# Column totals by one all-ones product, an earlier weight load and a finer deal of one block's second product, in an attention and mixture-of-experts kernel

## The chip, the cores and the metric

The kernel runs on one core of a Trainium2 chip. The metric is the device time of one execution in microseconds (us); lower is better. Most of what follows concerns three of the core's engines: TensorE (PE in the profile; its weight loads are shown apart, as PEld), VectorE (DVE) and ScalarE (ACT). PE multiplies matrices into PSUM; DVE and ACT do elementwise work and empty PSUM; POOL and SP here mostly issue DMA transfers (70 of POOL's 82 instructions in the profile before).

The mean granted TensorE clock of a run was 0.996 to 1.000. In the two stretches of time by which I judge below (stages A and B) it was 1.00 in the profiles before and after, and in every profile the first twenty 512-column products of stage A took 4.48 us and a pair of 384-column products in stage B 0.48 to 0.50 us, so it explains no difference there; in whole times it has a small share. Kernels that were timed in rounds have runs of the state "fast"; four kernels got a single look each, whose state is unknown, and I use their traces and not their whole times.

## The reference, cut to what matters

An attention with linear cost gives `x` (4608 tokens of 512 numbers). Then comes a mixture of eight experts, whose gates are made by the Sinkhorn normalisation. Eight times, rows and then columns of a 4608x8 matrix are scaled to fixed sums:

```python
logits = x @ w_gate
P = np.exp(logits - logits.max())
for _ in range(8):
    P /= P.sum(1, keepdims=True) + 1e-09
    P /= P.sum(0, keepdims=True) + 1e-09
    P *= N / E
out = np.zeros((N, D))
for e in range(E):
    h = np.maximum(x @ w1[e], 0.0)
    out += P[:, e:e + 1] * (h @ w2[e])
```

A row of `P` is one token, and a row sum needs only that token's eight numbers. A column sum runs over all tokens. On the chip the tokens lie over 128 partitions, 36 on each, so a column sum is first a sum within each partition (`colp`, 128x8) and then one across partitions, which this kernel gives to PE, as a product with ones.

## The kernel before: the parts that matter

The kernel has three stages. Attention and expert 0 run together over blocks of 512 tokens (blocks 0 to 6). In blocks 7 and 8 attention is over, expert 0 goes on, and the Sinkhorn normalisation runs beside it. From then on experts 1 to 7 run with a scheme of fewer products (sums of weights and of tokens are made by DVE so that seven products replace eight); there PE is nearly always busy (9.97 to 10.00 us of each 10 us window from 220 to 960 us, before).

The Sinkhorn normalisation is a generator: each `yield` hands back to the loop that issues PE's main work, so its pieces are dealt between other products. DVE works through its instructions in the order in which they are written (in the changed kernel a reciprocal that is written behind an add-relu starts at 195.41 us, behind the add-relu of 194.94, though its product began at 193.41; where it is written ahead, in scaled_at_once, it starts at 192.53, 0.43 us after its product), so where a `yield` stands decides what DVE has to do first.

```python
def sinkhorn():
    small = (W2[:, 0:E], W2[:, TCH - E : TCH])          # a borrowed PSUM bank
    for it in range(8):
        rs = ...; ve.reduce_sum(out=rs[:], in_=P_tok[:], axis=AX.X)
        rr = ...; ve.reciprocal(out=rr[:], in_=rs[:])
        yield
        ve.tensor_tensor(out=P_tok[:], ... rr ..., op=ALU.mult)
        colp = sk_pool.tile([P, E], FP32, name="colp")
        ve.reduce_sum(out=colp[:], ...)
        yield
        for step in tw_steps[it][:2]: step()            # sums of expert 1's weights
        yield
        tot_ps = small[0][0:1, :]                       # totals on one partition
        te.matmul(out=tot_ps, lhsT=ones_col[:], rhs=colp[:], start=True, stop=True)
        t2 = sk_pool.tile([1, E], FP32, name="t2")
        ve.reciprocal(out=t2[:], in_=tot_ps)
        for step in tw_steps[it][2:]: step()
        yield
        te.matmul(out=small[1], lhsT=scale_row[0:1, ...], rhs=t2[0:1, :], ...)  # to all
        ve.tensor_tensor(out=P_tok[:], ... small[1] ..., op=ALU.mult)
        yield
```

Sums of expert 1's first weights (`tw_steps`, four sets of four DVE instructions) ride along in iterations 3 to 6. In blocks 7 and 8, by slots of one 128-row product, and then in the fills of expert 1's first groups, the pieces are dealt so:

```python
for j in range(B - 1, NJ):                        # blocks 7 and 8
    tiles = halves(hT, w0, ...)                   # second product, each tile in 2 parts
    for slot in range(NS):
        if slot < FT: ffn1(hT, w0, j, [slot])     # first product
        elif j < NJ - 1: next(tiles)              # block 7: its second product too
        else: break
        ...
        if j == NJ - 1:                           # block 8
            if slot == 0: sums_x = x_sums(1, xs_first[1])
            next(sums_x, None)                    # four sums of tokens, for unit 1
        ... balanced(...)                         # pieces of Sinkhorn

def start_fill():                                 # 28 fills in expert 1's first groups
    if k_fill % 7 in (0, 3): next(tiles, None)    # block 8's second product
    if k_fill % 6 != 1: balanced(1)               # one piece of Sinkhorn
    k_fill += 1
```

When the last part of a tile is done, ACT or DVE, in turn, copies the 128x512 result from PSUM to `acc`.

## Time and profile before

| | before |
|---|---|
| median of 4 runs (those of the first comparison) | 983.02 us |
| profiled span | 980.3 us |
| PE busy | 967.1 us, 99% |
| DVE, ACT busy | 82%, 58% |

The first part of the page gives each engine's busy time, its share of the span and its instructions; the fourth part gives the chain of work that ended last, by engine:

```profile
PE 967.1 (99%) x7871; PEld 674.9 (69%) x7871; DVE 806.6 (82%) x1834; ACT 564.3 (58%) x1262; POOL 60.6 (6%) x82
...
PE 94%; DVE 2%; ACT 2%; DMA 1%; POOL 0%; issue 0%; ACTq 0%; SPq 0%; POOLq 0%
```

PE bounds the kernel nearly everywhere. What is left are the gaps on PE. From 222 us on there are hardly any before the last 20 us, so the change can win only in the hand-over to expert 1. I cut that hand-over in two by marks that every version has. Stage A runs from the first gate product of block 7 (`p_ps<-wg,xT`) to the first marking product (`copied_ps<-xT`, made when a PSUM bank is lent). Stage B runs from there to the second marking product. The start of both is the start of a record on PE's timeline, so the durations are exact to a few hundredths.

Lines of PE's timeline of the kernel before follow. The columns are start, length, engine, line, operation, output and inputs, shapes, count; in brackets stands the idle time before, and what ended it.

```profile
165.64 0.65 PE L109 MATMUL p_ps<-wg,xT 128*128 128x8 f16 x20
...
188.82 0.38 PE L109 MATMUL copied_ps<-xT 128*128 128x512 f16 x1
...
193.60 0.48 PE L109 MATMUL h_ps<-S,w1e 128*128 128x384 f16 x2 [0.41 <-ACT u L109]
...
199.62 0.20 PE L109 MATMUL copied_ps<-colp,ones_col 128*1 128x8 f32 x2 [1.20 <-DVE colp L109]
...
204.79 0.20 PE L109 MATMUL copied_ps<-colp,ones_col 128*1 128x8 f32 x2 [0.78 <-DVE colp L109]
...
210.41 0.38 PE L109 MATMUL copied_ps<-xT 128*128 128x512 f16 x1
```

Stage A takes 188.82 - 165.64 = 23.18 us, stage B 210.41 - 188.82 = 21.59 us. In B, PE waits 1.20 and 0.78 us for `colp`, DVE's sums within partitions. Two more waits for ACT (0.41 shown, and 0.24 at 210.1, both for `u`, a copy of an intermediate sum that ACT takes out of PSUM) and one of 0.15 in A make 2.78 us in both stages.

### The profile page before, as it was taken

What the parts mean: (1) busy time and instruction counts of PE and PEld (TensorE: products, weight loads), DVE (VectorE), ACT (ScalarE), POOL (GpSimd) and SP (SyncE); (2) the same over time, 40 slices, a digit from 0 to 9 for tenths busy, and PEclk for the clock granted to TensorE, in tenths of its full rate; (3) what the DMA queues carried; (4) which work ended last, traced back from release to release, by engine and by line L of the source; (5) the groups of instructions that cost most, each with busy time, mean ns of one, the idle gap of its engine ahead of it and who ended that gap; (6) DMA issues with size and microseconds to landing.
All of it is one profiled execution on the core that took longest, in us unless ns stands there. A gap on an engine that the chain in (4) does not pass through costs nothing.

```text
span 980.3 us, 20270 instructions
## 1 busy us (share of the span) xinstructions
PE 967.1 (99%) x7871; PEld 674.9 (69%) x7871; DVE 806.6 (82%) x1834; ACT 564.3 (58%) x1262; POOL 60.6 (6%) x82
## 2 busy tenths in 40 slices
PE   9999999989999999999999999999999999999997
PEld 6545444457777777777777777777777777777775
DVE  7767774788989888988888888988888888988887
ACT  5767665467776555555555555555555555555551
POOL 6231110010000000000000000000000000000001
PEclk9999999999999999999999999999999999999999
DMA  9999881730113400223103401223103401104435
GB/s 165 184 158 172 150 134 28 145 65 33 42 33 68 93 25 25 60 59 66 49 25 69 92 25 28 63 58 66 46 25 76 85 25 34 40 26 120 127 87 129
DMA packets 80336, 73.54 MB, mean 75 GB/s; under 512 B 33264, under 2 KB 72176, under 8 KB 80240
## 3 DMA queue, kind: packets, MB, share of 16 engines
q0 software_dynamic: 27232, 30.94, 20.2%
q1 hardware_dynamic: 52768, 41.06, 16.9%
q8 instruction: 61, 1.00, 0.4%
q14 instruction: 35, 0.29, 0.1%
q10 hardware_dynamic: 240, 0.26, 0.1%
HBM read 83.12 MB, written 12.98 MB: 98 GB/s over the span
## 4 chain that ended last, share of the span: by engine, by line
PE 94%; DVE 2%; ACT 2%; DMA 1%; POOL 0%; issue 0%; ACTq 0%; SPq 0%; POOLq 0%
PE rows_ps L109 34%; PE h_ps L109 28%; PE copied_ps L109 11%; PE p_ps L109 11%; PE y_ps L109 6%; PE small_ps L109 4%; DMA acc_hi<-q_p 1%; ACT hT L109 0%; ACT acc_lo L109 0%; DVE acc_hi L927 0%; POOL hs_last L942 0%; DVE P_tok L109 0%; DMA out_dram<-acc_lo 0%; DVE colp L109 0%; ACT u L109 0%
## 5 line engine op out<-in xcount | busy, mean ns | idle before, releaser
L927 DVE SCALAR_TENSOR_TENSOR acc_lo<-rows_ps,P_tok,acc_lo 128x512 f32<-128x512 f32 (+1 forms) x322 | 203.0, 639 | 74.4 <-PE rows_ps L109 74.3
L109 PEld LDWEIGHTS <-H 128*128 128x128 f16 x2080 | 203.0, 98 | 83.1 <-issue 1.2
L863 ACT CAST u<-h_ps 128x384 f16<-128x384 f32 x288 | 137.6, 478 | 131.2 <-PE h_ps L109 131.2
L109 PEld LDWEIGHTS <-w1e 128*128 128x128 f16 x1632 | 156.4, 98 | 66.4 <-issue 6.3
L857 DVE CUSTOM_DVE_ANT_0 H<-p_ps,u 128x384 f16<-128x384 f32 x329 | 180.8, 549 | 7.0 <-PE p_ps L109 6.6
L109 PEld LDWEIGHTS <-hs 128*128 128x128 f16 x1500 | 146.5, 98 | 56.2
L109 PE MATMUL h_ps<-S,w1e 128*128 128x384 f16 x672 | 164.1, 326 | 1.1 <-ACT u L109 0.9
L109 PE MATMUL p_ps<-xT,T 128*128 128x384 f16 x672 | 164.1, 326 | 0.1
L109 PE MATMUL rows_ps<-V,H 128*128 128x256 f16 x1000 | 150.0, 273 | 0.7 <-DVE acc_hi L927 0.7
L109 PE MATMUL h_ps<-xT,w1e 128*128 128x384 f16 (+1 forms) x616 | 150.0, 350 | 0.1
L109 PE MATMUL rows_ps<-w2e,hs 128*128 128x256 f16 x1000 | 150.0, 273 | 0.0
L895 ACT ACTIVATE H<-h_ps 128x384 f16<-128x384 f32 x144 | 70.6, 490 | 95.1 <-PE h_ps L109 95.1
L109 PEld LDWEIGHTS <-T 128*128 128x128 f16 x1008 | 98.1, 98 | 29.3 <-issue 2.8
L109 PE MATMUL rows_ps<-w2e,H 128*128 128x256 f16 (+1 forms) x568 | 91.2, 285 | 0.0
L876 ACT COPY copied_ps<-h_ps 128x384 f32<-128x384 f32 x144 | 67.5, 469 | 35.3 <-PE h_ps L109 35.3
L886 ACT ACTIVATE H<-copied_ps 128x384 f16<-128x384 f32 x144 | 70.8, 492 | 20.4 <-PE copied_ps L109 20.4
L109 PE MATMUL h_ps<-S,T 128*128 128x384 f16 x336 | 81.8, 325 | 0.3 <-ACT copied_ps L109 0.3
L109 PE MATMUL copied_ps<-xT,w1e 128*128 128x384 f16 x336 | 82.1, 326 | 0.0
L109 PE MATMUL copied_ps<-w2e,H 128*128 128x256 f16 x504 | 75.5, 272 | 0.0
L109 PE MATMUL rows_ps<-V,hs 128*128 128x256 f16 x500 | 75.0, 272 | 0.0
L927 DVE SCALAR_TENSOR_TENSOR acc_lo<-copied_ps,P_tok,acc_lo 128x256 f32<-128x256 f32 x126 | 60.0, 476 | 0.5
L927 DVE SCALAR_TENSOR_TENSOR acc_hi<-rows_ps,P_tok,acc_hi 128x512 f32<-128x512 f32 (+1 forms) x56 | 41.2, 736 | 20.5 <-PE rows_ps L109 19.7
(147 smaller groups left out, 950.0 us busy)
## 6 DMA issues: line engine op xcount, KB each, us to landing
S<-x_saved SPq DMA_DIRECT2D x108, 192.0 KB, 2.4
out_dram<-acc_lo SPq DMA_DIRECT2D x62, 128.0 KB, 2.4
w1e<-in_moe_w_dram POOLq DMA_DIRECT2D x7, 1024.0 KB, 8.9
w2e<-in_moe_w_dram POOLq DMA_DIRECT2D x7, 1024.0 KB, 9.7
q_ld<-in_q_dram POOLq DMA_DIRECT2D x16, 288.0 KB, 6.4
k_ld<-in_k_dram POOLq DMA_DIRECT2D x16, 288.0 KB, 8.2
v_ld<-in_v_dram POOLq DMA_DIRECT2D x16, 288.0 KB, 9.4
x_saved<-S SPq DMA_DIRECT2D x18, 192.0 KB, 1.9
```

The source lines that it names most:

```text
L109: i = getattr(self.engine, name)(*args, **kwargs)
L857: latest = ve._custom_dve(TENSOR_ADD_SAT, out=out, in0=ps[:, 0:TU], in1=t[:], s0=FP32_MAX, s1=0.0)
L863: se.copy(out=t[:], in_=ps[:, 0:TU])
L876: se.copy(out=Y[:, 0:TU], in_=X[:, 0:TU])
L886: se.activation(out=h11, in_=Y[:, 0:TU], func=AF.Relu)
L895: se.activation(out=h12, in_=X[:, 0:TU], func=AF.Relu)
L927: ve.scalar_tensor_tensor(out=a, in0=rows, scalar=P_tok[:, g, self.e : self.e + 1], in1=a, op0=ALU.mult, op1=ALU.add,)
```

## The change

It has three parts, with three intents. The totals are made with a 128x128 matrix of ones, so that every partition has them at once: one product per iteration instead of two, and no reciprocal on a single partition in between. Expert 1's weights take the place of the input buffers, which come free long before the buffer `hT` that they replaced until now; so their sums can be made two iterations earlier. The last block's second product is dealt in quarters of a tile and not in halves. The diff, cut to its core:

```diff
     with ExitStack() as p1:
-        hA = p1.enter_context(tc.tile_pool(name="hA", bufs=1))
-        cs_pool = p1.enter_context(tc.tile_pool(name="cs_pool", bufs=1))
         ld = p1.enter_context(tc.tile_pool(name="ld", bufs=4))
         ...
+        cs_pool = p1.enter_context(tc.tile_pool(name="cs_pool", bufs=1))
+        hA = p1.enter_context(tc.tile_pool(name="hA", bufs=1))
 ...
-        scale_row = const.tile([1, 2, P], FP32, name="scale_row")
+        ones_all = const.tile([P, P], FP32, name="ones_all")
+        ve.memset(ones_all[:], 1.0)
 ...
-            tot_ps = small[0][0:1, :]
-            te.matmul(out=tot_ps, lhsT=ones_col[:], rhs=colp[:], start=True, stop=True)
-            t2 = sk_pool.tile([1, E], FP32, name="t2")
-            ve.reciprocal(out=t2[:], in_=tot_ps)
+            te.matmul(out=total, lhsT=ones_all[:], rhs=colp[:], start=True, stop=True)
             for step in tw_steps[it][2:]:
                 step()
             yield
-            te.matmul(out=small[1], lhsT=scale_row[...], rhs=t2[0:1, :], ...)
-            ve.tensor_tensor(out=P_tok[:], in0=P_tok[:], in1=small[1]..., op=ALU.mult)
+            t2 = sk_pool.tile([P, E], FP32, name="t2")
+            ve.reciprocal(out=t2[:], in_=total)
+            ve.scalar_tensor_tensor(out=P_tok[:], in0=P_tok[:], scalar=<N/E or N/E/XS>,
+                in1=t2[:]..., op0=ALU.mult, op1=ALU.mult)
 ...
-        tw, tw_steps[3 + i] = w1_steps(w_next, i)
+        tw, tw_steps[1 + i] = w1_steps(w_next, i)
 ...
-        tiles = halves(hT, w0, [...])
+        tiles = dealt(hT, w0, [...], 2 if j < NJ - 1 else 4)
 ...
-        if k_fill % 7 in (0, 3):
+        if k_fill % 7 in (0, 2, 3, 5):
             next(tiles, None)
```

More of the change, by code (lines that the diff above doesn't have):

```diff
@@ L310 @@
         ve.memset(ones_col[:], 1.0)
-        scale_row = const.tile([1, 2, P], FP32, name="scale_row")
-        ve.memset(scale_row[:, 0, :], float(N) / float(E))
-        ve.memset(scale_row[:, 1, :], float(N) / float(E) / XS)
+        ones_all = const.tile([P, P], FP32, name="ones_all")
+        ve.memset(ones_all[:], 1.0)
         eps_row = cs_pool.tile([1, 32], FP32, name="eps_row")
@@ L1023, in sinkhorn @@
     def sinkhorn():
-        small = (W2[:, 0:E], W2[:, TCH - E : TCH])
+        total = W2[:, 0:E]
         for it in range(8):
@@ L1050, in sinkhorn @@
             yield
-            te.matmul(
-                out=small[1], lhsT=scale_row[0:1, 1 if it == 7 else 0, :], rhs=t2[0:1, :],
-                start=True, stop=True,
-            )
-            ve.tensor_tensor(
+            t2 = sk_pool.tile([P, E], FP32, name="t2")
+            ve.reciprocal(out=t2[:], in_=total)
+            ve.scalar_tensor_tensor(
                 out=P_tok[:], in0=P_tok[:],
-                in1=small[1].unsqueeze(1).to_broadcast([P, NG, E]), op=ALU.mult,
+                scalar=float(N) / float(E) / (XS if it == 7 else 1.0),
+                in1=t2[:].unsqueeze(1).to_broadcast([P, NG, E]),
+                op0=ALU.mult, op1=ALU.mult,
             )
@@ L1063, in balanced, with dealt @@
             next(balance, None)
-    def halves(hT, w, tiles):
+    def dealt(hT, w, tiles, parts):
         for i, (c0, g) in enumerate(tiles):
-            for part in range(2):
+            for part in range(parts):
                 ffn2(
                     hT, w, c0, g, rows2[i % 3][:],
-                    range(part * FT // 2, (part + 1) * FT // 2),
+                    range(part * FT // parts, (part + 1) * FT // parts),
                 )
@@ L1101 @@
         hT = next_h()
-        tiles = halves(hT, w0, [(ts * P, j * TCH // P + ts) for ts in range(TCH // P)])
+        tiles = dealt(
+            hT, w0, [(ts * P, j * TCH // P + ts) for ts in range(TCH // P)],
+            2 if j < NJ - 1 else 4,
+        )
         for slot in range(NS):
```

## The prediction

> **What bounds the kernel.** TensorE. The page of the kernel before has PE busy 99% of 980.3 us at a granted clock of 0.999; the chain that ended last is 94% PE. From 222 to 960 us every 10 us window shows PE at 9.97 to 10.00, and the change touches nothing there. All it can win lies at the hand-over from attention and expert 0 to expert 1, 163 to 215 us. PE's timeline there has seven idle gaps, 3.36 us together:
>
> - 2.13 us wait for DVE's part of the Sinkhorn normalisation (0.15 at 186.8, 1.20 at 199.6, 0.78 at 204.8);
> - 0.41 us at 193.6 waits for ACT's snapshot `u`, behind the copy of a finished tile to `acc_hi`;
> - 0.82 us at 210 to 214 waits for ACT, which then multiplies gates.
>
> **What the change does there.**
>
> 1. *Totals.* Each of 8 iterations has a 128x1 f32 product (0.12 us on the chain) and a 1x128 one (0.31 us); after each the next four 512-column products take 0.97 us, not 0.86. The first pair goes: (0.12 + 0.11) x 8 = 1.8 us of PE. The other will load 128x128 f32 weights. [...] I keep the 182 ns that the trace shows for the 1x128 load (80 ns for 128x1). A PE-DVE-PE trip goes too; DVE's reciprocal (192 ns) and multiplication (451 ns) should keep their size.
> 2. *Weights.* Expert 1's load lies in bytes that the last attention inputs free, not under `hT`. Their last DVE readers run at 140 to 145 us; now the load issues at 166.8. It should issue at 141 to 146 and land by about 156, where DMA is little used. By itself this saves nothing: the first weight sums start at 184.5, after landing. It lets the sums move from iterations 3 to 6 to 1 to 4. Each set is 0.28 + 0.29 + 0.23 + 0.27 = 1.07 us of DVE, so some 2 to 2.5 us leave 189 to 206 us, where DVE is nearly full. I estimate an iteration there at 2.65 us of Sinkhorn, 1.1 of add-relu and part of a 0.69 copy, some 4.0 us, against 4.1 of PE work; with the sums it was about 5. That is the 1.2 and 0.8 us of wait.
> 3. *Quarters.* The same products as 16 pieces of 0.43 us instead of 8 of 0.86. It evens PE's filler between a column sum and its total, and moves the tile copies from a group's fourth fill to its sixth, where ACT's snapshot isn't waiting.
>
> **Sum on the critical path.** Small products 1.8 us, DVE waits 2.13 to about 0.6 (1.5 us), ACT's copy about 0.2; the 0.82 us of gates stay. Some 3.3 us, or 0.3%. I predict 979.7 us, range 978.0 to 982.0. Faster by over 2%: 0.005; within 2%: 0.985; slower: 0.01.
>
> **What would show each step right.** Eight pairs of f32 products instead of sixteen, at about 0.3 us each. POOL's issue of `w1e` near 141 us, weight sums starting near 172 us, none after about 190. PE's waits for `colp` under 0.7 us in total. No tile copy ahead of a PE wait for `u`. After 222 us everything as before, 3 us earlier.
>
> **What would make it wrong.** The 128x128 f32 load or product costing more than the 1x128 one; the early load delaying the last transposes by DMA (3.4 us to landing) until the denominators at 149 us wait; weight sums in block 7 delaying DVE's evictions; the load still waiting for the attention stage's end, so that DVE stalls on it at 172 us; the four gates on ACT moving to a worse place.

## The result, and the profile after

The median fell from 983.02 us to 981.12 us (four runs each, 980.48 to 981.30 after, 982.31 to 985.69 before). The ratio is 0.9975, with a 95% interval of 0.9955 to 0.9994. Ratios here are the mean time of one kernel's runs over the mean time of the other's runs of the same rounds, so not quite the ratio of the medians that I quote. The gain of the medians is 1.9 us where I had predicted 3.3; the time is inside the predicted range, and the interval of the ratio leaves room for a gain of 0.6 to 4.4 us.

The same lines as before, from the page of the changed kernel:

```profile
PE 964.4 (99%) x7855; PEld 674.2 (69%) x7855; DVE 807.1 (82%) x1833; ACT 565.2 (58%) x1262; POOL 60.6 (6%) x82
...
PE 88%; DMA 4%; DVE 3%; issue 2%; ACT 1%; POOL 1%; POOLq 0%; ACTq 0%; SPq 0%
```

The chain's shares moved, but this is not the change at work in stages A and B: ahead of 66 us the chain now runs through early loads (`k_ld`, `w1e`, `w2e`). It does so in weights_alone (below) too, which is not faster. PE is busy 99% in both.

And from PE's timeline of the changed kernel, both gate and marking products and the waits in between:

```profile
165.98 0.64 PE L109 MATMUL p_ps<-wg,xT 128*128 128x8 f16 x20
...
187.44 0.38 PE L109 MATMUL copied_ps<-xT 128*128 128x512 f16 x1
...
189.77 0.39 PE L109 MATMUL copied_ps<-colp,ones_all 128*128 128x8 f32 x2 [1.20 <-DVE colp L109]
...
193.41 0.39 PE L109 MATMUL copied_ps<-colp,ones_all 128*128 128x8 f32 x2 [0.32 <-DVE colp L109]
...
198.25 0.39 PE L109 MATMUL copied_ps<-colp,ones_all 128*128 128x8 f32 x2 [0.74 <-DVE colp L109]
...
202.68 0.39 PE L109 MATMUL copied_ps<-colp,ones_all 128*128 128x8 f32 x2 [0.74 <-DVE colp L109]
...
208.64 0.38 PE L109 MATMUL copied_ps<-xT 128*128 128x512 f16 x1
```

Stage A takes 187.44 - 165.98 = 21.46 us, so 1.72 less. Stage B takes 208.64 - 187.44 = 21.20 us, so only 0.39 less. Together that is 2.11 us. (The rest after the second mark takes 770.2 us, against 769.9 before.) And PE's waits for `colp`, which I had expected under 0.7 us, are now 1.20 + 0.32 + 0.74 + 0.74 = 3.00 us, more than the 1.98 of before. The prediction of the total came out, but its account of stage B did not. The experiments ask why.

One thing first, because it decides how the experiments can be read. Whole times scatter by more than the change. Part of that comes from one transfer: near 72 us PE waits for a DMA that transposes queries and lands late: 5.1 to 8.2 us from issue to landing in the seven profiles whose DMA view from 60 to 76 us I read, where the two other transposes took 3.2 to 3.4 us and loads of 288 KB 5.9 to 11.8 us. Here is that wait in two kernels whose source is the same up to block 7 (the view of PE's waits: who waits for whom, in total, times, longest), first in the changed kernel and then in the one called "x_sums_early" below:

```profile
PE small_ps L109 <- DMA acc_hi<-q_p: 0.8, 1, 0.8
```

```profile
PE small_ps L109 <- DMA acc_hi<-q_p: 2.4, 1, 2.4
```

Over the profiled runs this wait was between none and 2.4 us, and stage A began between 165.4 and 169.5 us. Another part is the clock: in x_sums_early it was 0.59 from 76 to 80 us, after that wait, and from one block's gate products to the next this kernel took 20.15 us (77.69 to 97.84) where the changed one took 19.54. In no_quarters the clock was 0.73 in the same four us. (The mean over the run was 0.998 in both, against 1.000 in the profiled run of the changed kernel.) The longest runs of the kernel before in the later rounds, 986.16 and 988.30 us, had mean clocks of 0.997 and 0.996, and ratios of whole times contain that too. Stages A and B do not share that scatter: the changed kernel, run again later, gave 21.46 and 21.20 us, the same to the hundredth. So I judge effects of under 2 us by these stages, and use the whole time only where several rounds were run.

### The profile page after: what moved, and what is told of

Read it like the earlier page. It is cut to its first block, busy times and chain, and to the rows that moved or that the text cites. A ratio compares the mean times of both kernels' runs of the same rounds, so it can differ in the third digit from the quotient of the medians.

```text
span 978.8 us, 20237 instructions
## 1 busy us (share of the span) xinstructions
PE 964.4 (99%) x7855; PEld 674.2 (69%) x7855; DVE 807.1 (82%) x1833; ACT 565.2 (58%) x1262; POOL 60.6 (6%) x82
## 4 chain that ended last, share of the span: by engine, by line
PE 88%; DMA 4%; DVE 3%; issue 2%; ACT 1%; POOL 1%; POOLq 0%; ACTq 0%; SPq 0%
PE rows_ps L109 33%; PE h_ps L109 26%; PE p_ps L109 11%; PE copied_ps L109 11%; PE y_ps L109 4%; PE small_ps L109 3%; DMA k_ld<-in_k_dram 1%; DMA w2e<-in_moe_w_dram 1%; DMA w1e<-in_moe_w_dram 1%; DMA acc_hi<-q_p 1%; DVE P_tok L109 1%; DVE colp L109 0%; POOL q_ld L202 0%; DVE rs L109 0%; DVE acc_hi L926 0%
```

## The experiments

All twelve runs of this section gave correct results. Stage durations in us, with PE's waits in A and in B (those that the timeline marks on PE; a weight load that comes too late costs PE time as well, about 0.26 us by my estimate under product_twice, and is not among them):

| kernel | A | waits in A | B | waits in B | A + B |
|---|---|---|---|---|---|
| before | 23.18 | 0.15 | 21.59 | 2.63 | 44.77 |
| after | 21.46 | 0 | 21.20 | 3.28 | 42.66 |
| totals_alone | 21.21 | 0 | 21.85 | 3.77 | 43.06 |
| weights_alone | 23.31 | 0.28 | 21.59 | 2.62 | 44.90 |
| quarters_alone | 23.18 | 0.16 | 20.79 | 1.47 | 43.97 |
| no_weights | 21.20 | 0 | 21.26 | 3.32 | 42.46 |
| no_quarters | 21.46 | 0 | 22.37 | 4.29 | 43.83 |
| product_twice | 22.13 | 0 | 21.63 | 2.73 | 43.76 |
| scaled_at_once | 20.95 | 0 | 20.39 | 2.65 | 41.34 |
| x_sums_early | 21.62 | 0.45 | 19.45 | 1.76 | 41.07 |
| both | 21.51 | 0.34 | 19.06 | 1.35 | 40.57 |
| both_f16 | 21.10 | 0.47 | 18.31 | 1.35 | 39.41 |
| both_f16_no_weights | 20.46 | 0 | 19.68 | 2.73 | 40.14 |

Two theories stand against each other. The theory of load is the one that I predicted with: in stage B, DVE is full, and what is taken off DVE comes out of PE's waits. The theory of place says that DVE is not full there (busy 16.4 of 21.6 us before, 16.2 of 21.2 after, by the windows view of stage B), but works in written order, and that what matters is which instruction stands ahead of the Sinkhorn pieces and what that instruction waits for.

### Each part alone

**totals_alone**: the first part of the diff on the kernel before, nothing else.

> The kernel before with the all-ones totals alone. Stages are read from the PE timeline: A from the first gate product of block 7 to the first marking product (before 23.18 us, after 21.46), B from that mark to the second (before 21.59, after 21.20). If a product pair dropped from an iteration is worth 0.40 us of PE, as stage A of the changed kernel suggests (1.72 us in four iterations), and not the 0.23 us that I predicted, A is 21.4 to 21.6 here. In B four more iterations drop 1.6 us of products; if the saving comes back as waits for DVE's column sums, B is 21.0 to 21.6 and the waits for colp exceed the 1.98 us of before. The rival, that B has slack and the products count there too, gives B near 20.0.

Stage A fell to 21.21 us, more than I had expected; B rose to 21.85 us. The waits for `colp` in B were 2.8 us (the longest 1.60). Timed over three rounds it was 981.21 us in the median, ratio to before 0.9974 (0.9959 to 0.9989), as good as the whole change. So the totals part gains in A and returns its gain in B as waits.

**weights_alone**: only the order of the buffers and the move of the sums.

```diff
-        hA = p1.enter_context(tc.tile_pool(name="hA", bufs=1))
-        cs_pool = p1.enter_context(tc.tile_pool(name="cs_pool", bufs=1))
         ld = p1.enter_context(tc.tile_pool(name="ld", bufs=4))
         ...
+        cs_pool = p1.enter_context(tc.tile_pool(name="cs_pool", bufs=1))
+        hA = p1.enter_context(tc.tile_pool(name="hA", bufs=1))
...
-        tw, tw_steps[3 + i] = w1_steps(w_next, i)
+        tw, tw_steps[1 + i] = w1_steps(w_next, i)
```

> The kernel before with the buffers' order and the weight sums moved to iterations 1 to 4 alone. A stays at 23.0 to 23.4. Theory of place (stage B waits because DVE, in order, reaches the next scaling only behind an add-relu that waits for PE): taking weight sums out of B gives little, B 21.1 to 21.6. Theory of load, the one of my prediction (DVE is full in B): B falls by about 1.2 us, to 20.4, and the waits for colp to under 0.8.

B stayed at 21.59 us with the same waits of 1.20 and 0.78 us; A rose by 0.13. The load did go out early, at 147.74 us; that just brought nothing. The theory of load has fallen for this kernel. DVE's timeline of the kernel before shows why. These are its instructions ahead of the 1.20 us wait (PE waits until 199.62); `H<-p_ps,u` is an add-relu, which adds `u` to a sum that PE has made and cuts off what is negative:

```profile
195.02 0.27 DVE L109 TENSOR_TENSOR T<-w1e,T 128x256 f16<-128x256 f16 x1
195.87 0.56 DVE L109 CUSTOM_DVE_ANT_0 H<-p_ps,u 128x384 f16<-128x384 f32 x1 [0.58 <-PE p_ps L109]
196.35 0.44 DVE L109 TENSOR_TENSOR P_tok<-P_tok,copied_ps 128x288 f32<-128x288 f32 x1
196.82 0.45 DVE L109 TENSOR_REDUCE rs<-P_tok 128x36 f32<-128x288 f32 x1
197.31 0.38 DVE L109 RECIPROCAL rr<-rs 128x36 f32<-128x36 f32 x1
197.80 0.69 DVE L109 COPY acc_hi<-rows_ps 128x512 f32<-128x512 f32 x1
198.41 0.45 DVE L109 TENSOR_TENSOR P_tok<-P_tok,rr 128x288 f32<-128x288 f32 x1
198.90 0.67 DVE L109 TENSOR_REDUCE colp<-P_tok 128x8 f32<-128x288 f32 x1
```

The last sum of weights is over at 195.3, and then DVE idles 0.58 us. It waits for PE's product of the add-relu. From there the chain to the end of the column sum takes 3.70 us (195.87 to 199.57), and a part of it is not Sinkhorn's: the copy of a finished tile to `acc_hi` (0.69 us; PE ends the tile's last half at 197.8), behind which the scaling and the column sum are written. Taking weight sums away before the idle time only lengthens the idle time: in weights_alone it is 1.42 us at the same place.

**quarters_alone**: only the finer deal of block 8's second product.

```diff
-            for part in range(2):
+            for part in range(parts):          # 4 in block 8
...
-        if k_fill % 7 in (0, 3):
+        if k_fill % 7 in (0, 2, 3, 5):
```

> The kernel before with the last block's second product in quarters alone. A unchanged, 23.0 to 23.4. My prediction says that the filler gets more even and the 0.41 us wait for the snapshot u goes: B 21.0 to 21.3. The other theory: a quarter holds only 0.43 us of PE work before the first total of stage B, where a half holds 0.86, so a wait for colp appears there (0.2 to 0.6 us) and B is 21.4 to 21.9.

B fell to 20.79 us, better than both theories had it: the tile is done two fills later, its copy stands behind the column sum, and the wait of 1.20 us is gone (what is left for `colp` is 0.38 and 0.78, and 0.31 us at 201.6 for the reciprocal `t`, ahead of which the copy now stands). By whole time it is at the edge of clear: ratio 0.9984, interval 0.9967 to 1.0001.

### Each part taken out of the change

**no_weights**: the changed kernel with the second part undone.

> The changed kernel with the buffers' order and the weight sums put back (iterations 3 to 6). The part alone left stage B at 21.59 us to the hundredth, so it was worth nothing on the kernel before. Theory of place: in the changed kernel DVE idles 1.11 and 1.28 us in B behind column sums, and the sums of weights fall into just these gaps, so B stays at 21.1 to 21.6 us (after: 21.20). Theory of load (what I predicted): about 2.1 us of DVE work come back into B, and B rises to 22.2 to 23.0.

B was 21.26 us, as the theory of place expected; A was 21.20. So without this part the changed kernel is 0.20 us quicker in the two stages. The waits only lie elsewhere (0.66, 0.30, 0.74 and 1.34 us for `colp`).

**no_quarters**: the changed kernel with the third part undone.

> The changed kernel with the last block's second product in halves again. With the totals alone B was 21.85 us and the longest wait for colp 1.60; if the quarters are what removes that wait (the copy of a finished tile stands ahead of the column sum in DVE's order) and the weights add nothing, B is 21.7 to 22.0 here, A stays at 21.2 to 21.6. If the parts interact otherwise, B stays near 21.2.

B was 22.37 us, beyond the expected range: the quarters are worth 1.17 us inside the change, against 0.80 alone. The wait of 1.60 us is back: DVE's copy of a tile (at 200.25) stands ahead of the scaling again, and before that DVE idles 1.55 us at an add-relu that waits for PE.

### What one small product costs

**product_twice**: the same product made a second time.

```diff
             te.matmul(out=total, lhsT=ones_all[:], rhs=colp[:], start=True, stop=True)
+            te.matmul(out=total, lhsT=ones_all[:], rhs=colp[:], start=True, stop=True)
```

> The changed kernel with each all-ones product made twice (same result). It measures one product where PE waits for nothing, in stage A with four of them. If it costs the 0.42 us that I took from the 1x128 product, A rises by 1.7 us to 23.1; if it costs 0.14 to 0.28 us, as the changed kernel's timeline suggests, A rises by 0.6 to 1.1 us, to 22.0 to 22.6.

Stage A rose by 0.67 us for four more products, so 0.17 us each, not the 0.42 us that I had booked for the remaining product. The weight loads show the reason. First the kernel before, then the changed one (PEld with PE's products, same columns):

```profile
170.54 0.09 PEld L109 LDWEIGHTS copied_ps<-colp,ones_col 128*1 128x1 f32 x2 [0.42 <-DVE xT L109]
...
171.64 0.29 PEld L109 LDWEIGHTS copied_ps<-t,scale_row 1*128 1x128 f32 x2 [0.42 <-issue]
171.64 0.38 PE L109 MATMUL copied_ps<-t,scale_row 1*128 1x8 f32 x2
```

```profile
170.58 0.41 PEld L109 LDWEIGHTS copied_ps<-colp,ones_all 128*128 128x128 f32 x2
170.80 0.28 PE L109 MATMUL copied_ps<-colp,ones_all 128*128 128x8 f32 x2
...
184.60 0.30 PEld L109 LDWEIGHTS copied_ps<-colp,ones_all 128*128 128x128 f32 x2 [0.48 <-DVE colp L109]
184.61 0.39 PE L109 MATMUL copied_ps<-colp,ones_all 128*128 128x8 f32 x2
```

In the traces each of these f32 products is two pairs of load and product (the x2 above). In the kernel before, the load unit idled 0.42 us ahead of either small load, and the load of 1x128 began at 171.64 together with its product; that of 128x1 began at 170.54 and its product at 170.55. The loads of all sixteen small products of that kernel began within 0.01 us of their products, the first although `colp` had been done at 168.68. In the changed kernel the 128x128 load begins at 170.58 and its product at 170.80, and the next load follows at 170.83: 0.22 of the two loads' 0.41 us run under the product before. That the 128x128 load would take as long as the 1x128 one was my assumption, and it held: 188 ns against 182 ns. What I had missed is that the load can run in part under the product before. It did so only where `colp` was there: `colp` was done at 169.01 for the load at 170.58 and at 173.93 for that at 175.04 (product at 175.25). In the other six iterations, although it loads nothing but ones, the load began within 0.01 us of its product, 0.05 to 0.06 us after the end of `colp`. Where PE waits too, the product takes 0.25 us (189.77 to the next record at 190.02) and not 0.14 (170.80 to 170.94). In stage A two of the four loads come too late in this way, though the timeline marks no wait on PE: at 179.90 and at 184.60 above the load unit has idled 0.53 and 0.48 us for `colp`. What that costs can be estimated from no_weights, where of these two only the first comes too late: its A is 21.20 us and not 21.46, so a product with a late load costs about 0.26 us more, 0.40 and not 0.14.

### What stands ahead of the scaling

**scaled_at_once**: DVE's scaling written directly behind the product.

```diff
             te.matmul(out=total, lhsT=ones_all[:], rhs=colp[:], start=True, stop=True)
-            for step in tw_steps[it][2:]:
-                step()
-            yield
             t2 = sk_pool.tile([P, E], FP32, name="t2")
             ve.reciprocal(out=t2[:], in_=total)
             ve.scalar_tensor_tensor(...)
+            for step in tw_steps[it][2:]:
+                step()
             yield
+            yield
```

> The changed kernel with the reciprocal and the scaling written right behind the product of totals, not two fills later. In the changed kernel's timeline DVE sits idle 1.11 us at 193.8 and 1.28 us at 202.6 with the totals ready, because an add-relu that waits for PE comes first. Theory of place: PE's waits for colp in B fall from 3.0 us to 0.8 to 1.8, B from 21.2 to 19.4 to 20.2, the whole time to 979.2 to 980.3. Theory of load (DVE's amount of work in B sets it): the work is the same, so B stays at 21.0 to 21.4 and the time at 981.

B fell from 21.20 to 20.39 us, a little short of the expected 19.4 to 20.2 but well below what the theory of load allows, with the same work for DVE. A fell to 20.95. The median was 979.83 us, ratio to before 0.9957 (0.9940 to 0.9974). The waits for `colp` fell from 3.00 to 2.04 us, less than expected. One of them shows the mechanism. In the changed kernel the totals were ready soon after 193.41, but an add-relu was written ahead of the reciprocal and waited for PE:

```profile
193.28 0.55 DVE L109 CUSTOM_DVE_ANT_0 H<-p_ps,u 128x384 f16<-128x384 f32 x1
194.94 0.56 DVE L109 CUSTOM_DVE_ANT_0 H<-p_ps,u 128x384 f16<-128x384 f32 x1 [1.11 <-PE p_ps L109]
195.41 0.20 DVE L109 RECIPROCAL t<-copied_ps 128x8 f32<-128x8 f32 x1
195.65 0.46 DVE L109 SCALAR_TENSOR_TENSOR P_tok<-P_tok,t 128x288 f32<-128x288 f32 x1
```

DVE idles 1.11 us, the reciprocal starts at 195.41, 2.0 us after the start of the product, and PE's next product waits 0.74 us (at 198.25 above). In this version the reciprocal goes first, and this wait is gone (in B one of 0.61 us for ACT is new, at 203.82); from DVE's and then PE's timeline of scaled_at_once:

```profile
191.97 0.55 DVE L109 CUSTOM_DVE_ANT_0 H<-p_ps,u 128x384 f16<-128x384 f32 x1
192.53 0.21 DVE L109 RECIPROCAL t<-copied_ps 128x8 f32<-128x8 f32 x1
...
193.63 0.56 DVE L109 CUSTOM_DVE_ANT_0 H<-p_ps,u 128x384 f16<-128x384 f32 x1 [0.40 <-PE p_ps L109]
```

```profile
192.10 0.39 PE L109 MATMUL copied_ps<-colp,ones_all 128*128 128x8 f32 x2 [0.23 <-DVE colp L109]
...
196.21 0.39 PE L109 MATMUL copied_ps<-colp,ones_all 128*128 128x8 f32 x2
```

In both traces DVE keeps the written order. The kernel fixes this order when it is built, so what DVE would do without that was not shown.

**x_sums_early**: the four sums of unit 1's tokens (2.2 us of DVE) moved from block 8's first slots to block 7's slots 7 to 10. Block 7 and the tokens' earlier readers allow it.

```diff
             if j == B - 1 and slot:
-                next(sums_x, None)
-            if j == NJ - 1:
-                if slot == 0:
+                if slot == 7:
                     sums_x = x_sums(1, xs_first[1])
                 next(sums_x, None)
```

> The changed kernel with the four sums of unit 1's tokens (2.2 us of DVE) moved from the start of block 8 to the second half of block 7, where DVE idles. Theory: the first wait of stage B (1.20 us at 189.8) is there because these sums stand ahead of the reciprocal on DVE (186.9, though the product was done at 185.0); without them that wait falls to 0 to 0.2 us and B to 19.9 to 20.5, A 21.2 to 21.6. Rival: the wait comes from the quarters alone, which leave 0.43 us less PE work ahead of the first product; then it falls by no more than a few tenths, for DVE's iteration itself would be the limit.

The 1.20 us wait at the start of B is gone, the 0.32 us wait behind it as well, and B is 19.45 us, below the expected range; A paid 0.16 us. The rival is refuted: the iteration itself was no limit. (This kernel got one look; `both`, below, shows the same two waits gone.) In the changed kernel's DVE timeline, the sums stand ahead of the reciprocal whose product had begun at 184.61:

```profile
184.99 0.55 DVE L109 TENSOR_TENSOR S<-S,xT 128x768 f16<-128x768 f16 x1
185.58 0.56 DVE L109 TENSOR_TENSOR S<-xT,S 128x768 f16<-128x768 f16 x1
186.06 0.55 DVE L109 TENSOR_TENSOR xT<-xT 128x768 f16<-128x768 f16 x1
186.52 0.28 DVE L109 TENSOR_TENSOR w1e<-w1e 128x256 f16<-128x256 f16 x1
186.73 0.28 DVE L109 TENSOR_TENSOR T<-w1e,T 128x256 f16<-128x256 f16 x1
186.93 0.20 DVE L109 RECIPROCAL t<-copied_ps 128x8 f32<-128x8 f32 x1
```

So the 1.20 us of before and the 1.20 us of after are different waits of the same length: the first was behind a tile's copy, the second behind sums of tokens. The second delay was there in the kernel before too (its reciprocal of that iteration ended late, at 186.7, and PE waited 0.15 us for it), but PE reached the next total later then. All three parts have a share in uncovering it: the first wait in B is 0.25 us with the totals alone, 0.76 in no_quarters (totals and weights), 0.66 in no_weights (totals and quarters) and 1.20 with all three. The quarters took the first wait away and helped to uncover the second.

### The edits together

**after_again** is the changed kernel, as a measure on the same chip for the last three.

> The changed kernel once more, as a measure for the three others on the same chip. Stages A and B should repeat 21.46 and 21.20 us within 0.05; the whole time over the kernel before 0.997 to 0.999.

Both stages repeated exactly. Median 980.68 us of 6 runs, ratio to before 0.9965 (0.9949 to 0.9982), slightly under what I had written.

**both**: scaled_at_once and x_sums_early together.

> The changed kernel with the scaling right behind the product and unit 1's token sums in block 7, the two edits that each took waits out of stage B (B 20.39 and 19.45 us). If the two waits are separate, as the theory of place has it, the gains add: B 18.5 to 19.3, A 21.1 to 21.6, together 40.0 to 40.6 us against 42.66, and the time 2.0 to 2.6 us under the changed kernel's in the same rounds. If DVE's load is the limit by now, B stays at or over 19.4.

A + B is 40.57 us, 2.09 under the changed kernel and in the expected range. Alone the two edits had gained 1.32 and 1.59 us, 2.91 together, so the gains add in the main and not in full; in A nothing is left of the 0.51 us that scaled_at_once had won there. The whole time shows less than the expected 2.0 to 2.6 us: 979.81 against 980.68 us in the medians. Six runs spread from 979.30 to 985.83 us, and I count the whole time as unclear here (ratio to before 0.9974, interval 0.9948 to 1.0001).

**both_f16**: the ones and `colp` in f16.

```diff
-        ones_all = const.tile([P, P], FP32, name="ones_all")
+        ones_all = const.tile([P, P], F16, name="ones_all")
...
-            colp = sk_pool.tile([P, E], FP32, name="colp")
+            colp = sk_pool.tile([P, E], F16, name="colp")
```

> The same, with the all-ones weights and the column sums in f16, so that a product is one pass with a 98 ns load and not two passes with 188 ns loads each. The result changes by the rounding of 128 partial sums and should stay correct. With a product at about 0.06 us and not 0.14 to 0.25, A falls by 0.3 to 0.8 us and B by 0.2 to 0.8 us against the run with f32; less in B if the saving comes back as waits for DVE.

A fell by 0.41 and B by 0.75 us against `both`, as expected, and the result was correct. The 98 ns are the mean f16 load of 128x128 in the trace of the changed kernel, whose f32 loads took 188 ns. The 0.06 us for a product were my estimate; the trace shows one f16 record for a product, and 0.03 us from its start to the next record (170.63 to 170.66), against 0.14 to 0.25 us in f32. This is the quickest version: median 977.98 us of 6 runs, ratio to the kernel before 0.9940 (0.9921 to 0.9958), against 980.68 us and 0.9965 for the changed kernel in the same rounds. The two intervals still touch, so what is sure of the difference is the stages: 39.41 against 42.66 us.

**both_f16_no_weights**: the same without the weights' part.

> The same with the buffers' order and the weight sums as in the kernel before. If the weights' part is worth nothing here too, A and B together differ by under 0.3 us from the run with it. If, with the other waits gone, DVE's load has become the limit in stage B, B is 0.5 to 1.5 us longer here, and the weights' part pays at last.

A was 0.64 us shorter, B 1.37 us longer, together 0.73 us worse. So of the two alternatives that I had written the second came in, the theory of load: the sums of weights in B now cost PE's time (waits of 0.56 and 1.56 us for `colp`). The trace supports it: from 186.40 to 200.10 us DVE is busy 13.18 of 13.70 us, and its timeline marks no idle time until the column sum ahead of the second wait is done. Place decides while DVE has idle time between its instructions; once the other edits have used that up, the amount of work counts.

## Why the prediction was right or wrong

The total was right in its range (979.7 predicted, 978.0 to 982.0, measured 981.12), but that is in part luck, for two errors cancelled. In the two stages PE's work fell by 2.7 us (busy time 41.99 to 39.30), more than the 1.8 predicted, while PE's waits rose by 0.50 us (2.78 to 3.28) where they should have fallen by some 1.7. Point by point:

1. *Where the gain can lie.* Right. Nearly all of it is in stages A and B (2.11 us of the two profiles), and behind 222 us all is as it was.
2. *"The first pair goes: (0.12 + 0.11) x 8 = 1.8 us of PE."* The mechanism was right, the size too small. In A, without PE's waits, four iterations went from 23.03 to 21.46 us, so 0.39 us each and not 0.23; PE's busy time in B fell by 1.08 us more (18.96 to 17.88 in the windows view). The mis-sized term is the product that remains: I booked 0.42 us for it, its own 0.31 and a slower follower. In stage A it costs 0.14 us twice, where the 128x128 load runs in part under the product before, and by the estimate above about 0.40 us twice, where the load has to wait for `colp`: 0.27 us on average. With that the sum comes to 0.23 + 0.42 - 0.27 = 0.38 us, near the 0.39 measured. The second of two products costs 0.17 us (product_twice).
3. *"DVE waits 2.13 to about 0.6 (1.5 us)", by taking weight sums out of B.* This step failed. The waits for `colp` rose from 1.98 to 3.00 us. The part alone changed B by 0.00 us and cost 0.13 in A; within the change it cost 0.20 (0.26 in A, by the late load at 184.60, less 0.06 in B). I had added up DVE's work of an iteration, found 5 us against 4.1 of PE, and taken the difference for the wait. But DVE had idle time within the iteration; its work was late because of what stood ahead of it: the copy of a tile (before), sums of tokens and an add-relu that waits for PE (after). Only in the quickest version, where little idle time was left on DVE, was the part worth something (0.73 us).
4. *Quarters, "ACT's copy about 0.2".* Too small. They were worth 0.80 us alone and 1.17 within the change. The 0.41 us wait for ACT's snapshot `u` did go, but the larger effect is that DVE's copy of a tile no longer stands ahead of the column sum. I saw the copy's place for ACT and overlooked the same thing for DVE.
5. *The 0.82 us behind ACT's gates stay.* Right: 0.28 + 0.28 + 0.30 us after.
6. *Signs.* Eight pairs of small f32 products, right. Issue of `w1e` "near 141 us": it came at 147.28 us, a little late, and landed 8.1 us later; the first sum of weights started at 173.84 and the last at 190.37, about as said.

What stays open: why the loads of one row and of one column began within 0.01 us of their products (before) when the 128x128 load began 0.22 us ahead of its own (170.58, after), and the last wait of 0.74 us for `colp` in the quickest version, which no experiment took apart (DVE is busy 6.48 of the 6.75 us ahead of it, 192.55 to 199.30, which speaks for load and not for place there).

## What to carry to other kernels

When an engine that works in written order, as DVE did here, feeds the one that bounds, don't compare sums of work as long as it has idle time between its instructions; look on its timeline at what stands directly ahead of the late instruction, and what that was waiting for. Put the next link of a serial chain directly behind the one it depends on, and put work that has time (copies, sums for later) into stretches where the timeline shows that engine idle. And time saved on the bounding engine makes it arrive sooner at the next dependence, so check which wait that will uncover before counting the saving.
